# Pre-LN attention and gated feed-forward on one core: LN1 on ScalarE in three batches, exps of three and two banks, x of the tail loaded early

## The chip, the core and the metric

One core of a Trainium2 chip runs the kernel. Its engines work side by side, each through its own list of instructions in order: TensorE (PE) multiplies matrices out of the on-chip memory into eight accumulator banks, ScalarE (ACT) computes functions such as exp, VectorE (DVE) does elementwise work and reductions, GpSimd (POOL) general work, and SyncE (SP) issues DMA transfers. They wait for one another on semaphores. The metric is the device time of one execution in microseconds (us).

## The reference

x has 2,048 rows of 640 numbers in bf16. There are 32 heads of 20 numbers each; the feed-forward is 1,728 wide.

```python
h  = x + softmax_attention(layernorm(x) @ wqkv, heads=32, scale=20 ** -0.5) @ wo
n  = layernorm(h)
h2 = h + (gelu_tanh(n @ w_gate) * (n @ w_up)) @ w_down
layernorm(x) = (x - mean) / sqrt(var + 1e-5)
```

The softmax runs over all 2,048 keys. The output is h2.

## The kernel before

**The scheduler.** The kernel builds its whole program as a list of operations. Each has an engine, an assumed duration, a priority, its inputs and outputs and the accumulator banks that it takes and gives back (`op`, line 44). `schedule` (line 72) then plays the list through with the assumed durations: whenever an engine is free it takes the ready operation of the smallest priority number, and within one priority the one that was written first. What comes out is one fixed order per engine, and `emit` writes it down with the semaphore waits that it needs. On the chip each engine follows that order, whatever the true durations are. The priorities are `P_QK` 0 (scores, exps), `P_PV` 1 (products with the values), `P_EPI` 2 (epilogue) and `P_BG` 3 (everything in the background). Because all operations are recorded by one helper, most of them have line 257 in the profile.

**Head.** Sixteen tiles of 128 rows of x are loaded; `ln_stats` (line 400) takes mean and variance of each on DVE. After eight tiles `ln_rsqrt` (line 410) computes 1 / sqrt(var + eps) for them on DVE by a shift and two Newton steps. `ln_apply` (line 432) normalises a tile, five of each eight on POOL and three on DVE, into one of six slots. `transposes` (line 437) turns the tile on PE (five matmuls against the identity) and copies it out on ACT. POOL also spreads the weights of K and Q into padded arrays. `proj` (line 483) then makes K and Q of a group of four heads: five matmuls, a copy out of the bank, a square, a column sum on PE, for K a maximum, for Q a shift by half of K's maximum. `proj_v` makes the values. All of this has priority `P_BG`.

**Attention.** Queries come in five chunks: three of 512 (chunks 0 to 2) and two of 256 (chunks 3 and 4). Within a chunk the kernel goes over eight groups of four heads and over the keys. A tile is one bank of scores, 128 keys by 512 columns: one head and one key tile with 512 queries, or two key tiles with 256. `unit` (line 561) takes several tiles: the scores of all of them on PE, one exp over all their banks on ACT, and the products with the values on PE, which gather in bank 6. In chunk 0 a unit has two tiles, in banks 0, 1 or 2, 3 in turn; in all others three, in banks 0 to 2 or 3 to 5:

```python
units = [tiles[i:i + 2] for i in range(0, n2, 2)] + [tiles[i:i + 3] for i in range(n2, len(tiles), 3)]
```

In chunk 0 the projections of the other groups run in the background, in banks 7, 4 and 5. `epilogue` (line 614) takes a finished group out of bank 6, transposes it on PE in a background bank and divides by the sum of the exps.

**After a chunk.** `post` (line 637) takes the finished chunk: it loads x again (line 257, SP), transposes the attention output, multiplies by wo (line 478), adds x (line 655), normalises (LN2, again `ln_stats`, `ln_rsqrt`, `ln_apply`), and runs the feed-forward: gate and up matmuls (line 678), gelu from a tanh on ACT and several DVE steps, down matmuls (line 722), residual (line 726), store. It works in the background of the next chunk's units, at `P_BG` except for the first transposes, and in bank 7 alone. For the last chunk (`tail`) there is no next chunk: all eight banks are open and gelu is one ACT function (line 690).

Of the kernel before, what the change touches and what calls it, by code (L numbers as in the profile page):

```python
# [5 lines left out]
ACT = mybir.ActivationFunctionType  # L6
ALU = mybir.AluOpType
# [228 lines left out]
def bass_sequential_preLN__mha_block__glu_gated_geglu__prompt_kernel(  # L236
# [12 lines left out]
    with ExitStack() as es:  # L249
# [27 lines left out]
        rs = sb("rs", [128, NT], FP32)  # L277
        mu = sb("mu", [128, NT], FP32)
# [6 lines left out]
        qt_all = sb("qt_all", [128, NG, S])  # L285
# [10 lines left out]
        E_WORDS = 20820  # L296
# [26 lines left out]
        xn_p = carve(6 * D).rearrange("p (i d) -> p i d", i=6)  # L323
# [86 lines left out]
        def ln_rsqrt(t0, n, prio):  # L410
# [7 lines left out]
            d(I("tensor_scalar", sd16[:, 0:n], mv16[:, 0:n, 1], LN_EPS, None, ALU.add), ["mv16"], ["sd16"])  # L418
            d(I("tensor_copy", a, sd16[:, 0:n]), ["sd16"], ["nw0"])
            d(I("tensor_scalar", b.bitcast(I32), a.bitcast(I32), 1, None, ALU.logical_shift_right), ["nw0"], ["nw1"])  # L420
            d(I("tensor_copy", mu[:, t0:t0 + n], mv16[:, 0:n, 0]), ["mv16"], [("mu", t) for t in ts])
# [380 lines left out]
```

## Time and profile before

| | |
|---|---|
| runs, median (range) | 1109.22 us (1107.15 to 1115.55), three runs |
| the profiled execution | 1110.14 us, its span 1108.0 us |
| mean granted PE clock | 0.897 |
| ACT busy | 981.9 us, 89% |
| PE busy | 979.5 us, 88% |
| DVE busy | 438.2 us, 40% |
| POOL busy | 44.4 us, 4% |
| chain that ended last | ACT 55%, PE 37%, DVE 3%, POOL 3%, DMA 1% |

The span runs from the first to the last instruction of the profiled execution; the time of the execution lies a little above it. Busy is the time in which an engine works on at least one instruction. The chain that ended last is followed back from the last instruction, at each step to what released it. The granted clock is PE's, as a share of full speed.

### The profile page before, as it was taken

How to read it: one execution, taken by the hardware profiler on the slowest of the kernel's cores; microseconds unless marked ns; L12 is line 12 of the kernel's file. 1: busy time of each engine (PE TensorE's matmuls, PEld its weight loads, DVE VectorE, ACT ScalarE, POOL GpSimd, SP SyncE). 2: the span in 40 equal slices, each digit the busy share in tenths (PEclk: the TensorE clock that was granted, in tenths of full speed). 3: DMA queues.
4: the chain of work that ended last, by engine and by line, in shares of the span. 5: the costliest groups of instructions: out<-in, count | busy, mean ns of one | idle time of the engine just before them, and what ended most of it. 6: DMA issues, size and time to landing. Idle time of an engine off the chain costs nothing.

```text
span 1108.0 us, 16649 instructions
## 1 busy us (share of the span) xinstructions
PE 979.5 (88%) x7340; PEld 327.9 (30%) x7340; DVE 438.2 (40%) x917; ACT 981.9 (89%) x851; POOL 44.4 (4%) x47
## 2 busy tenths in 40 slices
PE   0599999999988998988899999988898989989768
PEld 0333332222222222331132222321132223333346
DVE  6344545555634555110035554110045554134532
ACT  0379999999889999999998999999999999999611
POOL 8700000000000000000000000000000000000000
PEclk9899999999978999995576999985589999998979
DMA  5000000000060000000000000000000000000000
GB/s 213 1 12 1 1 1 1 1 1 1 1 240 13 1 1 1 12 25 1 1 12 1 1 1 1 13 24 1 1 13 2 1 1 1 14 25 1 1 24 13
DMA packets 11832, 18.84 MB, mean 17 GB/s; under 512 B 688, under 2 KB 9840, under 8 KB 11760
## 3 DMA queue, kind: packets, MB, share of 16 engines
q1 hardware_dynamic: 11760, 17.78, 4.5%
q8 instruction: 57, 0.93, 0.4%
q14 instruction: 15, 0.12, 0.0%
HBM read 15.16 MB, written 2.62 MB: 16 GB/s over the span
## 4 chain that ended last, share of the span: by engine, by line
ACT 55%; PE 37%; DVE 3%; POOL 3%; DMA 1%; issue 0%; POOLq 0%; SPq 0%
ACT pts L257 53%; PE ps L257 17%; PE ps L478 10%; PE ps L678 4%; POOL rege L257 2%; ACT rege L257 2%; PE ps L513 2%; PE ps L722 2%; PE ps L624 1%; PE ps L441 1%; DMA rege<-in_A_wqkv_dram 1%; DVE rege L257 1%; POOL regw L257 1%; DVE rege L693 1%; DVE rege L709 0%
## 5 line engine op out<-in xcount | busy, mean ns | idle before, releaser
L257 ACT ACTIVATE pts<-ps 128x1536 bf16<-128x1536 f32 (+1 forms) x768 | 942.3, 1382 | 23.2 <-PE ps L257 19.9
L257 PE MATMUL ps<-qt_all,kt_all 32*128 32x512 bf16 (+1 forms) x2560 | 327.7, 374 | 55.7 <-ACT pts L257 53.2
L257 PE MATMUL ps<-pts,v_all 128*21 128x512 bf16 (+1 forms) x2560 | 286.5, 376 | 1.0 <-DVE osb L257 0.9
L678 PE MATMUL ps<-rege,regw 128*128 128x512 bf16 (+2 forms) x700 | 161.8, 350 | 18.8 <-DVE rege L693 6.5
L257 PEld LDWEIGHTS ps<-qt_all,kt_all 32*128 32x128 bf16 x2560 | 77.8, 93 | 309.7 <-ACT pts L257 237.2
L478 PE MATMUL ps<-regw 128*128 128x512 bf16 (+1 forms) x480 | 137.4, 368 | 0.0
L257 PEld LDWEIGHTS ps<-pts,v_all 128*21 128x21 bf16 x2560 | 65.8, 90 | 175.6 <-issue 164.6
L678 PEld LDWEIGHTS ps<-rege,regw 128*128 128x128 bf16 (+1 forms) x700 | 56.8, 101 | 86.8 <-issue 27.7
L722 PE MATMUL ps<-regw,rege 128*128 128x320 bf16 x448 | 80.6, 303 | 0.9 <-DVE rege L707 0.8
L257 DVE COPY osb<-ps 128x512 f32<-128x512 f32 (+1 forms) x40 | 23.3, 582 | 142.9 <-PE ps L257 142.9
L257 DVE SCALAR_TENSOR_TENSOR rege<-rege 128x512 bf16<-128x512 bf16 (+2 forms) x98 | 67.5, 689 | 20.9 <-ACT rege L257 19.3
L693 DVE CAST rege<-ps 128x512 bf16<-128x512 f32 (+1 forms) x49 | 33.8, 690 | 71.0 <-PE ps L678 70.8
L726 DVE TENSOR_TENSOR rege<-ps,rege 128x320 bf16<-128x320 f32 x32 | 15.7, 491 | 114.3 <-PE ps L722 114.2
L478 PEld LDWEIGHTS ps<-regw 128*128 128x128 bf16 x480 | 38.9, 101 | 57.1 <-issue 46.1
L709 DVE SCALAR_TENSOR_TENSOR rege<-rege,ps 128x512 bf16<-128x512 bf16 (+1 forms) x49 | 33.6, 686 | 46.5 <-PE ps L678 46.2
L722 PEld LDWEIGHTS ps<-regw,rege 128*128 128x128 bf16 x448 | 37.2, 98 | 37.3 <-issue 22.6
L447 ACT ACTIVATE regw<-ps 128x640 bf16<-128x640 bf16 x16 | 10.7, 703 | 39.8 <-PE ps L441 39.8
L441 PE MATMUL ps<-ident,rege 128*128 128x128 bf16 x80 | 10.8, 298 | 37.1 <-DVE mv L257 18.8
L257 ACT ACTIVATE rege<-rege 128x512 f32<-128x512 bf16 (+1 forms) x49 | 35.2, 719 | 8.7 <-DVE rege L257 8.5
L624 PE MATMUL ps<-identf,osb 128*128 128x128 f32 x128 | 33.5, 344 | 2.5 <-DVE osb L257 1.3
L524 DVE SCALAR_TENSOR_TENSOR qt_all<-ps,khalf,qt_all 128x512 bf16<-128x512 f32 x32 | 24.0, 750 | 21.1 <-PE ps L513 21.1
L540 DVE CAST v_all<-ps 128x320 bf16<-128x320 f32 x32 | 15.7, 492 | 42.0 <-PE ps L478 42.0
(62 smaller groups left out, 426.0 us busy)
## 6 DMA issues: line engine op xcount, KB each, us to landing
rege<-in_A_x_dram SPq DMA_DIRECT2D x4, 640.0 KB, 6.2
rege<-in_A_x_dram SPq DMA_DIRECT2D x16, 160.0 KB, 2.2
out_dram<-rege SPq DMA_DIRECT2D x16, 160.0 KB, 1.8
regw<-in_B_w_gate_dram SPq DMA_DIRECT2D x1, 2160.0 KB, 7.9
regw<-in_B_w_up_dram SPq DMA_DIRECT2D x1, 2160.0 KB, 12.8
regw<-in_B_w_down_dram SPq DMA_DIRECT2D x1, 2080.0 KB, 17.5
rege<-in_A_wqkv_dram SPq DMA_DIRECT2D x1, 1600.0 KB, 11.1
regw<-in_A_wqkv_dram SPq DMA_DIRECT2D x1, 800.0 KB, 12.5
```

What stands on the lines that cost most here:

```text
L257: return lambda eng: getattr(eng, method)(*args, **kwargs)
L441: op("pe", lambda eng, a=a: eng.transpose(bank16(bk, D)[:, 128 * a:128 * a + 128], src[:, a * 128:(a + 1) * 128], ident[:]), c_mm(128), pr ...
L478: yield op("pe", lambda eng, l=l, r=r, k=k: eng.matmul(bank(bk, n), l, r, start=(k == 0), stop=(k == len(steps) - 1)), c_mm(n), prio, read ...
L513: op("pe", lambda eng: eng.matmul(bank(b2), gm[:], sq[:, sqi, :], start=True, stop=True), c_mm(512), prio, reads=[("sq", sqi), "gq", "gqh" ...
L524: op("dve", lambda eng: eng.scalar_tensor_tensor(out=dst, in0=bank(b2), scalar=khalf[:, g:g + 1], in1=dst, op0=ALU.add, op1=ALU.add), c_dv ...
L540: op("dve", lambda eng: eng.tensor_copy(dst, src()), c_dve(320), prio, reads=[key], writes=[("v", kt, hf)], rel=[bk])
L624: op("pe", lambda eng, tt=tt: eng.transpose(bank(b2)[:, tt * 128:(tt + 1) * 128], osb[:, s, tt * 128:(tt + 1) * 128], identf[:]), c_mm(128 ...
L678: op("pe", lambda eng, a=a, f=f, fi=fi, mf=mf: eng.matmul(bank(bk)[0:mf, fi * nq:(fi + 1) * nq], w[:, a, f * 128:f * 128 + mf], hnT[:, a, ...
L693: op("dve", lambda eng, bg=bg, g16=g16, m=m: eng.tensor_copy(g16, bank(bg)[0:m, :]), c_dve(512), p, reads=[kg], writes=[("gb", i)], rel=[b ...
L709: fn = lambda eng, bu=bu, g16=g16, fv=fv, m=m: eng.scalar_tensor_tensor(out=fv, in0=g16, scalar=0.5, in1=bank(bu)[0:m, :], op0=ALU.mult, o ...
L722: op("pe", lambda eng, f=f, mf=mf, o=o, hf=hf, bk=bk: eng.matmul(bank(bk, 320), ha_f[0:mf, o:o + 128], wd[0:mf, f, hf * 320:(hf + 1) * 320 ...
L726: op("dve", lambda eng, bk=bk, tt=tt, hf=hf, i=i: eng.tensor_tensor(ob[:, i, hf * 320:(hf + 1) * 320], bank(bk, 320), h_sb[:, tt, hf * 320 ...
```

## The change

LN1 is done in three batches, of 4, 4 and 8 tiles. The square root of each batch is an ACT function, followed by a reciprocal on DVE and a product that gives minus mean over deviation. The first two batches are applied on ACT (one function with a scale and a bias per row), the third on DVE; POOL applies none. The slots for normalised tiles go from six to four. LN1, and K and Q of the first group of heads, have priority `P_EPI`.

Units of the last two chunks take three and two tiles in turn, in banks 0 to 2 and 3 to 4, and `post` and `epilogue` that run beside them have banks 7 and 5.

Q is stored by chunk, and the scratch of the gelu takes the place of chunk 0's Q; so `post` of chunk 0 also waits for that chunk's last scores. For the last chunk x is loaded once, into a buffer of its own, as soon as LN1 is done, and its part up to LN2 has priority `P_EPI`; LN2's Newton steps stay.

```diff
-        qt_all = sb("qt_all", [128, NG, S])
+        nm = sb("nm", [128, NT], FP32)
+        qt_all = sb("qt_all", [128, 4, NG, 512])
...
-        xn_p = carve(6 * D).rearrange("p (i d) -> p i d", i=6)
+        xn_p = carve(4 * D).rearrange("p (i d) -> p i d", i=4)
...
+        xr2 = carve(2 * D).rearrange("p (i s) -> p i s", i=2)
+        carve = carver(qt_all[:, 0, :, :].rearrange("p g s -> p (g s)"), NG * 512)
         th = carve(4 * 512).bitcast(FP32).rearrange("p (i s) -> p i s", i=2)
         zb = carve(2 * 512).rearrange("p (i s) -> p i s", i=2)
         gb = carve(2 * 512).rearrange("p (i s) -> p i s", i=2)
...
-        def ln_rsqrt(t0, n, prio):
+        def ln_rsqrt(t0, n, prio, need_nm=False):
...
+            if need_nm:
+                op("act", I("activation", sd16[:, 0:n], sd16[:, 0:n], ACT.Sqrt), 0.25, prio, reads=["sd16"], writes=["sd16"])
+                d(I("reciprocal", y, sd16[:, 0:n]), ["sd16"], rk)
+                d(I("scalar_tensor_tensor", out=nm[:, t0:t0 + n], in0=y, scalar=-1.0, in1=mu[:, t0:t0 + n],
+                    op0=ALU.mult, op1=ALU.mult), rk + [("mu", t) for t in ts], [("nm", t) for t in ts])
+                return
...
+            if eng == "act":
+                fn = I("activation", dst, src, ACT.Identity, bias=nm[:, t:t + 1], scale=rs[:, t:t + 1])
...
-        for i in range(2):
-            for t in range(8 * i, 8 * i + 8):
+        for t0, n, eng in ((0, 4, "act"), (4, 4, "act"), (8, 8, "dve")):
+            for t in range(t0, t0 + n):
                 ln_stats(x_sb[:, t, :], t, [f"x{t // 4}"], P_BG)
-            ln_rsqrt(8 * i, 8, P_BG)
-            for t in range(8 * i, 8 * i + 8):
-                eng = "pool" if t % 8 < 5 else "dve"
-                e_ops.append(ln_apply(eng, x_sb[:, t, :], xn_p[:, t % 6, :], ("xnp", t % 6), t, [f"x{t // 4}"], P_BG))
-                transposes(xn_p[:, t % 6, :], [("xnp", t % 6)], xnT[:, :, t * 128:(t + 1) * 128], ("xnT", t),
-                           ALLB, P_BG, "act")
+            ln_rsqrt(t0, n, P_EPI, True)
+            for t in range(t0, t0 + n):
+                e_ops.append(ln_apply(eng, x_sb[:, t, :], xn_p[:, t % 4, :], ("xnp", t % 4), t, [f"x{t // 4}"], P_EPI))
+                transposes(xn_p[:, t % 4, :], [("xnp", t % 4)], xnT[:, :, t * 128:(t + 1) * 128], ("xnT", t),
+                           ALLB, P_EPI, "act")
...
+        PAT = [((0, 1), (2, 3))] + [((0, 1, 2), (3, 4, 5))] * 2 + [((0, 1, 2), (3, 4))] * 2
...
+        while i < len(tiles):
+            pat = PAT[tiles[i][0]]
+            bs = pat[len(units) % 2]
+            units.append(tiles[i:i + len(bs)])
+            ubank.append(bs[0])
+            i += len(bs)
...
-            s0 = (2 if small else 3) * (u % 2)
+            s0 = ubank[u]
...
-            p = P_BG
+            p = P_EPI if tail else P_BG
...
-            first = tuple(e_ops) if c == 0 else ()
+            first = tuple(e_ops) + (last_qk0[0],) if c == 0 else ()
+            last = c == len(CHUNKS) - 1
...
-                op("sp", I("dma_start", xr[:, i, :], x_hbm[t * 128:(t + 1) * 128, :]), 0.08, p,
-                   writes=[("ob", i, 0), ("ob", i, 1)], sem=f"xr{i}", lat=2.5, after=first)
+                if not last:
+                    op("sp", I("dma_start", xr[:, i, :], x_hbm[t * 128:(t + 1) * 128, :]), 0.08, p,
+                       writes=[("ob", i, 0), ("ob", i, 1)], sem=f"xr{i}", lat=2.5, after=first)
+                elif tt == 0:
+                    op("sp", I("dma_start", xr2, x_hbm[q0:q0 + nq, :].rearrange("(i p) d -> p i d", p=128)), 0.08, p,
+                       writes=[("xr2", ii, jj) for ii in range(2) for jj in range(2)], sem="xr2", lat=2.5,
+                       after=tuple(e_ops))
...
+            p = P_BG
             hk = [("hnT", tt) for tt in range(nt)]
...
-        BG1 = (7,)
-        BG0 = (7, 4, 5)
+        BG = [tuple(b for b in (7, 5, 4) if b not in PAT[c][0] + PAT[c][1]) for c in range(len(CHUNKS))]
+        BG0 = BG[0]
...
-            proj("k", 0, c, PRO, P_BG, "act")
-        proj("q", 0, 0, PRO, P_BG, "act")
+            proj("k", 0, c, PRO, P_EPI, "act")
+        proj("q", 0, 0, PRO, P_EPI, "act")
...
-            post(c, ALLB if tail else BG1, tail)
+            post(c, ALLB if tail else BG[c + 1], tail)
```

## Rows read from the trace of the kernel before

**Rows 1.** Windows by stage: us, busy (instructions) by engine, granted PE clock, DMA

```profile
0.00:65.40 65.40, 27.98 (x155) 14.95 (x156) 31.22 (x104) 15.27 (x23) 44.44 (x47) 0.90 0.27 96
65.40:306.00 240.60, 238.99 (x1474) 71.48 (x1474) 128.47 (x231) 233.14 (x247) 0.00 (x0) 1.00 0.00 1
803.00:813.00 10.00, 10.00 (x96) 3.79 (x91) 2.46 (x6) 8.79 (x7) 0.00 (x0) 0.50 0.01 2
803.00:1042.90 239.90, 217.21 (x2530) 79.53 (x2525) 103.08 (x228) 236.51 (x189) 0.00 (x0) 0.96 0.02 7
1042.90:1108.00 65.10, 47.35 (x334) 32.36 (x332) 21.65 (x52) 9.13 (x14) 0.00 (x0) 0.87 0.05 16
```

**Rows 2.** Timeline of the head: start, us, engine, line, operation, count [idle before]

```profile
5.10 1.28 DVE L257 BATCH_NORM_STATS2 stats<-rege 128x6 f32<-128x320 bf16 x3 [1.36 <-DMA rege<-in_A_x_dram]
...
8.97 0.84 DVE L257 BATCH_NORM_STATS2 stats<-rege 128x6 f32<-128x320 bf16 x2
...
40.67 13.07 POOL L257 TENSOR_SCALAR rege<-rege,mu,rs 128x640 bf16<-128x640 bf16 x5 [4.90 <-DVE rs L257]
...
53.80 0.72 PE L441 MATMUL ps<-ident,rege 128*128 128x128 bf16 x5 [1.03 <-POOL rege L257]
...
54.55 1.90 ACT L447 ACTIVATE regw<-ps 128x640 bf16<-128x640 bf16 x3 [1.90 <-PE ps L441]
```

**Rows 3.** Timeline from the last normalised tile to the first exp

```profile
58.12 0.59 ACT L498 ACTIVATE qt_all<-ps 128x512 bf16<-128x512 f32 x1
...
60.40 0.69 ACT L495 ACTIVATE kt_all<-ps,e 128x512 bf16<-128x512 f32 x1 [1.68 <-PE ps L478]
...
61.12 0.42 DVE L257 TENSOR_TENSOR sq<-kt_all 128x512 bf16<-128x512 bf16 x1
...
62.03 0.69 DVE L516 TENSOR_REDUCE kmx<-ps 128x1 f32<-128x512 f32 x1
...
65.37 15.08 ACT L257 ACTIVATE pts<-ps 128x1024 bf16<-128x1024 f32 x16 [4.28 <-PE ps L257]
```

**Rows 4.** The chain that ended last, an undisturbed stretch: start, us, what

```profile
443.46 57.47 ACT pts L257 x43
```

**Rows 5.** Timeline of the tail

```profile
1045.18 0.32 DVE L632 TENSOR_TENSOR o_nat<-ps,rc 128x160 bf16<-128x160 f32 x1
...
1063.40 2.18 PE L722 MATMUL ps<-regw,rege 128*128 128x320 bf16 x14
...
1070.05 0.89 DVE L655 TENSOR_TENSOR rege<-ps,rege 128x320 bf16<-128x320 f32 x2 [2.38 <-DMA rege<-in_A_x_dram]
...
1072.14 0.17 DVE L257 CAST mv<-mv 128x4 bf16<-128x4 f32 x1
...
1074.73 0.80 DVE L257 TENSOR_SCALAR xn_t<-rege,mu,rs 128x640 bf16<-128x640 bf16 x2
...
1077.30 1.28 ACT L690 ACT_TABLE_LOAD   x1
...
1077.34 18.59 PE L678 MATMUL ps<-rege,regw 128*128 128x256 bf16 x140 [0.86 <-ACT rege L447]
```

**Rows 6.** Groups of the head: line, operation, count, busy, mean ns, idle before

```profile
L478 PE MATMUL ps<-regw 128*128 128x512 bf16 (+1 forms) x66 | 18.4, 420 | 0.0
```

**Rows 7.** The chain within the first chunk

```profile
106.56 0.65 PE ps L257 x6
107.21 0.32 PE ps L478
...
109.89 0.54 PE ps L478 x2
```

**Rows 8.** Groups of the tail

```profile
L678 PE MATMUL ps<-rege,regw 128*128 128x256 bf16 (+1 forms) x174 | 23.9, 300 | 4.9 <-ACT rege L257 2.6 <-ACT rege L447 0.9 <-DVE rege L709 0.8
...
L722 PE MATMUL ps<-regw,rege 128*128 128x320 bf16 x112 | 17.9, 308 | 0.8 <-DVE rege L707 0.8
```

**Rows 9.** Timeline where the first 256-query chunk begins

```profile
808.13 1.45 ACT L257 ACTIVATE pts<-ps 128x1536 bf16<-128x1536 f32 x1 [0.28 <-PE ps L257]
```

More of the change, by code (lines that the diff above doesn't have):

```diff
@@ L30 @@
     __slots__ = ("i", "eng", "fns", "dur", "lat", "prio", "deps", "succ", "nd", "ready",
-                 "acq", "rel", "sem", "start", "fin", "pos", "know")
+                 "acq", "rel", "sem", "tag", "start", "fin", "pos", "know")
 class Sched:
@@ L47, in op @@
         o.eng, o.dur, o.lat, o.sem = eng, dur, lat, sem
+        o.tag = writes[0] if writes else None
         o.fns = fns if isinstance(fns, list) else [fns]
@@ L418, in ln_rsqrt @@
             d(I("tensor_scalar", sd16[:, 0:n], mv16[:, 0:n, 1], LN_EPS, None, ALU.add), ["mv16"], ["sd16"])
+            d(I("tensor_copy", mu[:, t0:t0 + n], mv16[:, 0:n, 0]), ["mv16"], [("mu", t) for t in ts])
+            if need_nm:
[4 more added lines that the diff above has]
+                return
             d(I("tensor_copy", a, sd16[:, 0:n]), ["sd16"], ["nw0"])
             d(I("tensor_scalar", b.bitcast(I32), a.bitcast(I32), 1, None, ALU.logical_shift_right), ["nw0"], ["nw1"])
-            d(I("tensor_copy", mu[:, t0:t0 + n], mv16[:, 0:n, 0]), ["mv16"], [("mu", t) for t in ts])
             d(I("tensor_scalar", y.bitcast(I32), b.bitcast(I32), -1.0, RSQRT_MAGIC, ALU.mult, ALU.add), ["nw1"], rk)
@@ L483, in proj @@
         def proj(which, g, c, banks, prio, evac="dve"):
-            wp, all_, nm = (wk_pad, kt_all, "k") if which == "k" else (wq_pad, qt_all, "q")
+            wp, nm = (wk_pad, "k") if which == "k" else (wq_pad, "q")
             wkey = ("wkp" if which == "k" else "wqp") + ("0" if g == 0 else "")
-            dst = all_[:, g, c * 512:(c + 1) * 512]
+            dst = kt_all[:, g, c * 512:(c + 1) * 512] if which == "k" else qt_all[:, c, g, :]
             bk = Bank(*banks)
@@ L548, in bass_sequential_preLN__mha_block__glu_gated_geglu__prompt_kernel @@
             tiles += [(c, g, kb, j) for g in range(NG) for kb in range(NT // nk) for j in range(4)]
+        PAT = [((0, 1), (2, 3))] + [((0, 1, 2), (3, 4, 5))] * 2 + [((0, 1, 2), (3, 4))] * 2
         n2 = 64 * NG
-        units = [tiles[i:i + 2] for i in range(0, n2, 2)] + [tiles[i:i + 3] for i in range(n2, len(tiles), 3)]
+        units, ubank = [], []
+        i = 0
+        while i < len(tiles):
[4 more added lines that the diff above has]
+            i += len(bs)
         ends = []
@@ L559, in bass_sequential_preLN__mha_block__glu_gated_geglu__prompt_kernel @@
         pv_wait = []
+        last_qk0 = [None]
         def unit(u):
@@ L620, in epilogue @@
                reads=[("O", c, g)], writes=[("osb", s)], rel=[bk])
-            b2 = Bank(*(BG0 if c == 0 else BG1))
+            b2 = Bank(*BG[c])
             key = ("bk", sc_id())
@@ L637, in post @@
         def post(c, banks, tail):
-            p = P_BG
+            p = P_EPI if tail else P_BG
             q0, nq = CHUNKS[c]
             nt = nq // 128
-            first = tuple(e_ops) if c == 0 else ()
+            first = tuple(e_ops) + (last_qk0[0],) if c == 0 else ()
+            last = c == len(CHUNKS) - 1
+            xrb, xk = (xr2, "xr2") if last else (xr, "ob")
             ev = "act" if tail else "dve"
@@ L655, in post @@
                     op("dve", lambda eng, bk=bk, tt=tt, hf=hf, i=i: eng.tensor_tensor(
-                        h_sb[:, tt, hf * 320:(hf + 1) * 320], bank(bk, 320), xr[:, i, hf * 320:(hf + 1) * 320], ALU.add),
-                       c_dve(320), p, reads=[key, ("ob", i, hf)], writes=[("h", tt, hf)], rel=[bk], after=first)
+                        h_sb[:, tt, hf * 320:(hf + 1) * 320], bank(bk, 320), xrb[:, i, hf * 320:(hf + 1) * 320], ALU.add),
+                       c_dve(320), p, reads=[key, (xk, i, hf)], writes=[("h", tt, hf)], rel=[bk], after=first)
                 ln_stats(h_sb[:, tt, :], t, [("h", tt, 0), ("h", tt, 1)], p)
```

19 lines of the change are left out of this document (11 added, 8 removed).

## The prediction

> **What bounds the kernel now.** The page's totals have ScalarE (ACT) and TensorE (PE) each busy for nearly nine tenths of the span, and an average over unlike stages cannot say which limits, so I read the table by stage first [rows 1]. Until 65.4 us ACT is busy 15.3 us: no exp has started. From 65.4 to 306 (queries 0 to 511, exps of two banks) ACT works 233.1 of 240.6 us and PE 239.0. From 803 to 1042.9 (the two 256-query chunks) ACT works 236.5 of 239.9 us, PE 217.2. After the last exp 65.1 us remain, with ACT at 9.1 and PE at 47.4. So there are a head that waits, a stretch in which PE and ACT are level, one in which ACT leads and PE has 22.7 us idle, and a tail that waits.
>
> Next the order of time in the head: the chain runs through GpSimd (POOL). Five LN1 applies there take 13.07 us, in two such groups, and the last three transposed tiles are evacuated only at 54.55 + 1.90 = 56.45 [rows 2]. From there to the first exp at 65.37 it is a chain of small steps [rows 3]. In the middle the chain of waits is ACT's own: 43 exps of three banks in 57.47 us, 1.3365 each [rows 4]. In the tail PE first does the feed-forward left over from the chunk before, DVE waits for x, a chain of 14 short DVE operations follows, and the last feed-forward starts at 1077.34 [rows 5].
>
> **The change, part by part.** The sum is made against the profiled execution: span 1108.0, time 1110.14; the median of the three runs is 0.9 lower.
>
> *LN1 (removes ten POOL applies and the Newton steps).* When is the last tile normalised? DVE's statistics start at 5.1 us, when x lands, and nine halves (4.5 tiles) on it is 8.97: 0.86 us a tile [rows 2], so 13.8 for sixteen. Three square-root groups of five short DVE operations at 0.19, the pitch in the tail ((1074.73 - 1072.14) / 14 [rows 5]), add 2.8. Two squares and maxima of K (0.42 + 0.69 each [rows 3]), which now go ahead of statistics, add 2.2. The last group is ready at 5.1 + 13.8 + 2.8 + 2.2 = 23.9; a hop to ACT for the square root and back, 0.7, makes 24.6. Eight tiles follow at the pace of their slowest step, five transposes in about 0.7 (0.72 for five; evacuations three in 1.90 [rows 2]); the first also needs its apply, 0.5, and the last its evacuation, 0.7. So 24.6 + 0.5 + 8 x 0.7 + 0.7 = 31.4, instead of 56.45.
>
> An apply of 640 elements on ACT, with a scale and a bias read from memory, is not in the trace. Low end: an evacuation of 640 elements without them, 0.6 back to back. High end 0.8: K's evacuation with one such operand takes 0.69, Q's without one 0.59 [rows 3], so 0.1 an operand. I take 0.8, the nearer row. Eight are 6.4 us, 16 evacuations 9.6, K's and Q's 3: 19 us between about 10 and 34, which fits with little room. The ends move the head by 0 to 2 us.
>
> From the last tile on: five matmuls of Q's and K's width at 0.22 and hops are 1.3 us; from the last K evacuation at 60.40 to the first exp at 65.37 the trace has 4.97 [rows 3]. The 4 us between 56.45 and 60.40 were mostly other matmuls, which now stand behind. So the first exp comes at 31.4 + 1.3 + 5.0 = 37.7, say 38, instead of 65.4: **minus 27.4**. Ends: 33 and 46.
>
> Square root and exp bring a second function table. The one load that the trace shows amid the work takes 1.28 us and starts as ACT's earlier work ends, beside the first matmuls of the group whose results ACT waits for [rows 5]. One more, between Q's evacuation and the first exp, falls into a wait of 3 us or more: 0, at most 1.28. The Trainium skill (ScalarE: Activation LUTs, What ACT_TABLE_LOAD costs) has about 2.66 us for a switch with its drain against the row's 1.28; by its figure the uncovered end would be 1.4 us higher.
>
> *What PE did meanwhile.* By 65.4 it had done 66 projection matmuls [rows 6]; K and Q of the first group are 25 of them, so 41 others, mostly V, stood beside the POOL wait. At 0.155 us (14 of V's width in 2.18 [rows 5]) they are 6.4 us. In the shorter head about half may find room; the rest goes into the stretch after, where PE is level with ACT: **plus 3.5** (0 to 7).
>
> *Exps of 3 and 2 banks in turn.* 2,048 tiles make 768 exps now and 802 after, 34 more, all in the last two chunks. On ACT five tiles cost 1.3365 x 5/3 = 2.2275 now and 1.3365 + p after; the pace p of a two-bank exp lies between 0.89 (two thirds of 1.3365: no fixed part) and 0.94 (240.6 / 256, with PE in the way). I take the middle, 0.917: 102 pairs make 2.6 us (0 to 5). On PE a unit pays 0.65 for scores and products; a background burst takes 0.32 for one matmul and 0.54 for two, so 0.10 for the interruption [rows 7]. 34 units add 34 x 0.75 = 25.5 us against PE's idle of 22.7. ACT then wants 236.5 + 2.6 = 239.1, PE 217.2 + 25.5 = 242.7, just the longer: 242.7 for 239.9, **plus 3** (0 to 12).
>
> *Second bank for the background.* Now bank 7 alone serves the feed-forward and the epilogue's transposes, and a group waits for DVE to evacuate the one before. With bank 5 the next can start. But by the last paragraph PE has no idle left, so I count no faster background: 0, and about the same leftover at the last exp.
>
> *Tail.* Normalisation and output projection of the last chunk go ahead of the leftover. The chunk's own chain from the last exp at 1042.9: epilogue to 1045.5, 2.6; ten transposes 1.4, evacuations 1.3; ten projection matmuls 1.5; residual, statistics and square root 4.7 (1070.05 to 1074.73); applies 0.8, transposes 0.7, evacuation 0.7, hops 0.6: 14.3, against 1077.34 - 1042.9 = 34.4. Beyond that group's 140 matmuls and the last 56, PE still does 34 and 56 after the last exp [rows 8]: at 18.59 / 140 and 2.18 / 14 [rows 5] 4.5 + 8.7 = 13.2 us. With 4.4 of the chain's own PE work that overfills 14.3 by 3. So **minus 17** (0 if the leftover still goes first; 22 if it is gone and the group's slow first matmuls are too).
>
> *The x load* leaves SP's queue in the tail and is issued once, behind LN1; behind it stand only chunk 0's x and the weights, both wanted near 300 us. The DVE wait that it removes, 2.38 us [rows 5], is inside the 17. *Costed at nothing:* scratch moved into chunk 0's queries (its first user waits for that chunk's products anyway, which come after its scores); four slots instead of six for normalised tiles (a slot comes free with its transposes; without that cover the tile pitch grows by an apply, 8 x 0.5 = 4 us); Q's new order.
>
> Sum: -27.4 + 3.5 + 3 - 17 = -37.9. **1110.1 - 37.9 = 1072.2**; from the median 1071.3. I say 1072.
>
> **The rivals.**
> 1. *PE sets the pace of the last two chunks and the background falls behind.* For it: 25.5 us of new PE work against 22.7 of room. If 10 us are lost there and the tail stays: 1110 - 27.4 + 3.5 + 10 = 1096; with half the tail's gain 1088. Against it: two banks make fewer waits. The Trainium skill (TensorEngine Tiling (Array Packing), Key Properties) says that a change of tiling mode drains the engine, so that more, smaller units are more drains; by that rule this rival, and the bursts' fixed 0.10 agrees. Chance 0.20, at 1083 to 1097.
> 2. *Slower: PE's clock.* From 803 to 813, right after a stretch without background, the granted clock was 0.50, 1.2 GHz [rows 1], and a unit with a burst took 1.45 + 0.28 = 1.73 us, ACT waiting [rows 9]. If the last two chunks stay at that level, 204 units are 353 us instead of 240: 1110 + 113 - 41 = 1182. It decides from a mean of (240 + 41 + 11) / 204 = 1.43 us a unit, most of them at half clock. Against it: 0.96 over both chunks, and PE gets more to do, not less. Chance 0.04.
> 3. *The head stays.* A static order that puts a statistics step or an evacuation behind a wait of another engine could keep the first exp at 55; with rival 1's losses: 1110 - 10 + 5 - 5 = 1100. For it: sixteen tiles' work of ACT and DVE in order fills both. Against it: with POOL gone no single step is over 1 us. Chance 0.07.
> 4. *Better throughout:* first exp at 33, little lost in the middle, tail minus 22: 1110 - 32 + 3 - 22 = 1059 or less. Chance 0.09.
>
> **How the numbers follow.** The forecast (1060 to 1083) has 0.60. The range 1058 to 1092 takes it in, with over half of rival 1 and half of rival 4: some 0.78. Under 1% (11 us) a change can hardly be told from none: faster by more 0.90 (forecast, rivals 1 and 4, a little of 3), within it 0.05, slower 0.05.
>
> **What would show it.** POOL done near 23 us; the last normalised tile evacuated near 31, the first exp near 38; three table loads, the second before the first exp. Chunk 0's exps over 240 to 248 us. The last two chunks over 240 to 246 us, PE hardly idle. From the last exp to the end 48 us, the long feed-forward group starting 14 to 18 us in. Wrong would be a first exp after 46, last chunks over 250, a tail over 58.

## The result and the profile after

| | before | after |
|---|---|---|
| runs, median (range) | 1110.41 us (1107.15 to 1115.55), four runs | 1079.20 us (1077.46 to 1084.56), four runs |
| the profiled execution | 1110.14 us, span 1108.0 | 1080.92 us, span 1079.1 |
| mean granted PE clock | 0.897 | 0.899 |
| PE busy, ACT busy | 979.5, 981.9 us | 994.7, 995.2 us |

The ratio is 0.9723, with an interval from 0.9669 to 0.9777. The time lies within the range of 1058 to 1092 and 7 us above the 1072 forecast. The sum behind it is another matter: several of its terms were wrong, in both directions. The two profiled spans, cut at the first exp, at the end of each chunk's exps and at the last exp, give the terms one by one:

| stage | before | after | measured | forecast |
|---|---|---|---|---|
| head, to the first exp | 65.4 | 42.4 | -23.0 | -27.4 |
| chunk 0 | 249.4 | 244.2 | -5.2 | +3.5 |
| chunk 1 | 243.5 | 248.6 | +5.1 | 0 |
| chunk 2 | 242.3 | 243.5 | +1.2 | 0 |
| chunks 3 and 4 | 242.4 | 253.9 | +11.5 | +3 |
| tail, from the last exp | 65.1 | 46.6 | -18.5 | -17 |
| sum | 1108.0 | 1079.1 | -28.9 | -37.9 |

The windows of the kernel after, by those stages, answer to [rows 1]; the columns are the same (from, to, length; busy time and instructions of PE, PEld, DVE, ACT, POOL; granted clock; DMA share; GB/s):

```profile
0.00:42.40 42.40, 25.75 (x177) 14.50 (x178) 30.02 (x97) 22.81 (x35) 19.16 (x37) 1.00 0.44 147
42.40:286.60 244.20, 242.58 (x1496) 71.80 (x1494) 131.71 (x233) 242.08 (x256) 0.00 (x0) 1.00 0.01 3
286.60:535.20 248.60, 219.94 (x1394) 63.48 (x1394) 74.73 (x148) 238.52 (x186) 0.00 (x0) 0.82 0.09 32
778.70:911.70 133.00, 130.73 (x1266) 43.61 (x1266) 65.98 (x140) 124.91 (x117) 0.00 (x0) 0.89 0.01 4
911.70:1032.60 120.90, 117.62 (x1346) 47.80 (x1342) 42.10 (x98) 120.24 (x110) 0.00 (x0) 1.00 0.03 10
1032.60:1079.10 46.50, 36.77 (x273) 25.79 (x271) 16.26 (x43) 8.06 (x12) 0.00 (x0) 0.93 0.04 15
```

In chunk 3 PE is busy 130.73 of 133.0 us and ACT misses 8.1; in chunk 1 ACT misses 10.1 although PE is idle for 28.7, so there a wait of another kind sits. The head's timeline, which answers to [rows 2, 3], shows POOL gone from the chain and where the head lost the 4.4 us that the forecast had promised:

```profile
11.57 1.73 ACT L258 ACTIVATE rege<-rege,nm,rs 128x640 bf16<-128x640 bf16 x2 [0.72 <-DVE nm L258]
...
15.05 8.28 POOL L258 COPY regw<-rege 128x400 bf16<-128x400 bf16 x12 [1.55 <-DMA rege<-in_A_wqkv_dram]
...
17.32 2.56 PE L493 MATMUL ps<-regw 128*128 128x320 bf16 x9 [3.25 <-DMA regw<-in_A_wqkv_dram]
...
20.44 0.70 ACT L463 ACTIVATE regw<-ps 128x640 bf16<-128x640 bf16 x1 [4.01 <-PE ps L457]
21.04 0.20 ACT L258 ACTIVATE sd<-sd 128x4 bf16<-128x4 bf16 x1
21.27 0.18 DVE L258 RECIPROCAL rs<-sd 128x4 f32<-128x4 bf16 x1 [4.70 <-ACT sd L258]
...
29.78 2.94 DVE L258 TENSOR_SCALAR rege<-rege,mu,rs 128x640 bf16<-128x640 bf16 x8
30.76 4.88 ACT L463 ACTIVATE regw<-ps 128x640 bf16<-128x640 bf16 x8 [0.39 <-PE ps L457]
...
37.40 0.69 ACT L510 ACTIVATE kt_all<-ps,e 128x512 bf16<-128x512 f32 x1 [1.19 <-PE ps L493]
38.10 1.28 ACT L258 ACT_TABLE_LOAD   x1
42.37 1.02 ACT L258 ACTIVATE pts<-ps 128x1024 bf16<-128x1024 f32 x1 [2.98 <-PE ps L258]
```

Three engines stand for one transfer here. PE stands for 3.25 us, until 17.32, at a matmul of V (320 columns) whose weights have not landed, and the transposes that could run are behind it in PE's order. ACT waits 4.01 us for one of them, the second square root sits behind that evacuation on ACT, and DVE waits 4.70 us for the square root. From the last evacuation of K at 37.40 to the first exp at 42.37 it is 4.97 us, to the hundredth what [rows 3] had.

In the tail, the timeline that answers to [rows 5] has no wait for x, and the long feed-forward group starts 16.5 us after the last exp:

```profile
1034.73 0.32 DVE L658 TENSOR_TENSOR o_nat<-ps,rc 128x160 bf16<-128x160 f32 x1
...
1035.11 0.73 PE L457 MATMUL ps<-ident,o_nat 128*128 128x128 bf16 x10
...
1036.36 2.97 PE L493 MATMUL ps<-wo,rege 128*128 128x320 bf16 x20
...
1039.26 2.42 PE L756 MATMUL ps<-regw,rege 64*128 64x320 bf16 x15
...
1042.24 0.49 DVE L688 TENSOR_TENSOR rege<-ps,rege 128x320 bf16<-128x320 f32 x1
...
1046.53 0.80 DVE L258 TENSOR_SCALAR xn_t<-rege,mu,rs 128x640 bf16<-128x640 bf16 x2
...
1049.10 1.28 ACT L724 ACT_TABLE_LOAD   x1
1049.13 17.93 PE L712 MATMUL ps<-rege,regw 128*128 128x256 bf16 x140 [0.86 <-ACT rege L463]
...
1067.85 8.51 PE L756 MATMUL ps<-regw,rege 128*128 128x320 bf16 x56 [0.78 <-DVE rege L741]
```

After the last exp PE does 140 gate and up matmuls, all of them the last chunk's own, and 87 down matmuls, of which 31 are the chunk's before. In [rows 8] it was 34 and 56 left over. What removed that leftover is the question that the experiments answer.

### The profile page after: what moved, and what is told of

The parts are those of the page before. It is cut to its first block, busy times and chain, and to the rows that moved or that the text cites. A ratio compares the mean times of both kernels' runs of the same rounds, so it can differ in the third digit from the quotient of the medians.

```text
span 1079.1 us, 16678 instructions
## 1 busy us (share of the span) xinstructions
PE 994.7 (92%) x7340; PEld 330.8 (31%) x7340; DVE 435.1 (40%) x906; ACT 995.2 (92%) x897; POOL 19.2 (2%) x37
## 4 chain that ended last, share of the span: by engine, by line
PE 48%; ACT 46%; DMA 3%; DVE 3%; issue 0%; SPq 0%; DVEq 0%
ACT pts L258 44%; PE ps L258 23%; PE ps L493 11%; PE ps L712 6%; PE ps L756 3%; PE ps L457 2%; DMA rege<-in_A_x_dram 2%; ACT qt_all L258 2%; PE ps L528 2%; PE ps L650 2%; DMA regw<-in_A_wqkv_dram 1%; DVE qt_all L258 1%; DVE qt_all L727 1%; DVE rege L743 0%; SPq L258 0%
## 5 line engine op out<-in xcount | busy, mean ns | idle before, releaser
L258 PE MATMUL ps<-qt_all,kt_all 32*128 32x512 bf16 (+1 forms) x2560 | 342.6, 375 | 42.1 <-ACT pts L258 40.2
L258 PE MATMUL ps<-pts,v_all 128*21 128x512 bf16 (+1 forms) x2560 | 298.3, 377 | 0.5 <-DVE osb L258 0.4
L258 PEld LDWEIGHTS ps<-qt_all,kt_all 32*128 32x128 bf16 x2560 | 81.6, 93 | 302.1 <-ACT pts L258 212.4
L258 DVE COPY osb<-ps 128x512 f32<-128x512 f32 (+1 forms) x40 | 23.3, 582 | 141.2 <-PE ps L258 140.9
L258 DVE SCALAR_TENSOR_TENSOR qt_all<-qt_all 128x512 bf16<-128x512 bf16 (+2 forms) x98 | 67.2, 688 | 12.2 <-ACT qt_all L258 10.6
L727 DVE CAST qt_all<-ps 128x512 bf16<-128x512 f32 (+1 forms) x49 | 33.9, 691 | 69.0 <-PE ps L712 68.8
L760 DVE TENSOR_TENSOR rege<-ps,rege 128x320 bf16<-128x320 f32 x32 | 15.7, 492 | 111.3 <-PE ps L756 111.2
L743 DVE SCALAR_TENSOR_TENSOR rege<-qt_all,ps 128x512 bf16<-128x512 bf16 (+1 forms) x49 | 33.6, 687 | 44.3 <-PE ps L712 44.2
L493 PE MATMUL ps<-wo,rege 128*128 128x320 bf16 x160 | 32.2, 321 | 5.2 <-DVE rege L688 5.2
L258 ACT ACTIVATE qt_all<-qt_all 128x512 f32<-128x512 bf16 (+1 forms) x49 | 33.0, 674 | 1.0 <-DVE qt_all L258 0.8
L656 DVE RECIPROCAL rc<-ps 128x16 f32<-128x16 f32 (+1 forms) x40 | 9.5, 236 | 59.5 <-PE ps L650 59.5
L688 DVE TENSOR_TENSOR rege<-ps,rege 128x320 bf16<-128x320 f32 x32 | 15.7, 492 | 39.4 <-PE ps L493 32.2
```

What stands on the lines that cost most here:

```text
L258: return lambda eng: getattr(eng, method)(*args, **kwargs)
L493: yield op("pe", lambda eng, l=l, r=r, k=k: eng.matmul(bank(bk, n), l, r, start=(k == 0), stop=(k == len(steps) - 1)), c_mm(n), prio, read ...
L688: op("dve", lambda eng, bk=bk, tt=tt, hf=hf, i=i: eng.tensor_tensor(h_sb[:, tt, hf * 320:(hf + 1) * 320], bank(bk, 320), xrb[:, i, hf * 32 ...
L727: op("dve", lambda eng, bg=bg, g16=g16, m=m: eng.tensor_copy(g16, bank(bg)[0:m, :]), c_dve(512), p, reads=[kg], writes=[("gb", i)], rel=[b ...
L743: fn = lambda eng, bu=bu, g16=g16, fv=fv, m=m: eng.scalar_tensor_tensor(out=fv, in0=g16, scalar=0.5, in1=bank(bu)[0:m, :], op0=ALU.mult, o ...
L760: op("dve", lambda eng, bk=bk, tt=tt, hf=hf, i=i: eng.tensor_tensor(ob[:, i, hf * 320:(hf + 1) * 320], bank(bk, 320), h_sb[:, tt, hf * 320 ...
```

## Experiments

Each was timed against the kernel before on the same chip, and each has a profile. Stage lengths are those of one profiled execution, and they differ somewhat where nothing was changed: in the kernels below that leave the changed head alone it takes 41.6 to 42.4 us, and chunk 2 takes 238.2 to 244.9 in the kernels without the filler of experiment 5. The single repairs of experiments 3 to 5 gain 3 to 5 us on the kernel after, with intervals that overlap its own (0.9669 to 0.9777). So they are judged by the wait that each removes from the trace, and not by the total alone.

**1. One part at a time.** Three kernels start from the kernel before and take one part of the change each.

LN1 alone:

```diff
-            for t in range(8 * i, 8 * i + 8):
-                eng = "pool" if t % 8 < 5 else "dve"
+        for t0, n, eng in ((0, 4, "act"), (4, 4, "act"), (8, 8, "dve")):
+            ln_rsqrt(t0, n, P_EPI, True)
```

> The kernel before with the LN1 part alone (batches of 4, 4 and 8, square roots and two batches on ACT, priority for LN1 and the first K and Q). Theory A, the stages add up: first exp at 42 us, chunk 0 about 244 us long, the last two chunks 242 and the tail 65 as before; in all 28 us less, 1082. Rival B, the head's gain is given back in chunk 0 by projections that were not done early: first exp at 42, chunk 0 longer than 249, 1090 or more.

Measured: 1084.2 us, ratio 0.9748 (0.9693 to 0.9804). Stages: head 42.0, chunk 0 244.2, chunk 1 244.0, chunks 3 and 4 242.1, tail 67.1. Theory A holds: the head and the shorter chunk 0 are the LN1 part's; chunk 1 is not lengthened by it. The tail, whose code is the same as before, takes 67.1 instead of 65.1, so a difference of 2 us there says little by itself.

The tail part alone (priority of the last `post`, x loaded early into its own buffer):

```diff
-            p = P_BG
+            p = P_EPI if tail else P_BG
...
+                    op("sp", I("dma_start", xr2, x_hbm[q0:q0 + nq, :].rearrange("(i p) d -> p i d", p=128)), 0.08, p,
```

> The kernel before with the tail's part alone (priority of the last chunk's normalisation and output projection, its x loaded early). Theory A: the tail goes from 65 to about 47 us without the second background bank, everything else as before, 1092. Rival C, the tail is short only because two banks leave less over: it stays above 58 us, 1103 or more.

Measured: 1107.72 us, ratio 0.9977 (0.9950 to 1.0005); tail 62.6 instead of 65.1: no clear gain in all, and rival C holds (above 58 us, 1103 or more). The wait for x of 2.38 us is gone from the trace and little else. The tail's timeline says why the priority did nothing:

```profile
1044.10 0.32 DVE L633 TENSOR_TENSOR o_nat<-ps,rc 128x160 bf16<-128x160 f32 x1
...
1050.54 1.92 PE L687 MATMUL ps<-rege,regw 128*128 128x256 bf16 x10 [2.63 <-ACT rege L257]
1052.40 1.25 PE L442 MATMUL ps<-ident,o_nat 128*128 128x128 bf16 x10
...
1061.70 0.49 DVE L735 TENSOR_TENSOR rege<-ps,rege 128x320 bf16<-128x320 f32 x1 [1.75 <-PE ps L731]
1062.22 0.49 DVE L663 TENSOR_TENSOR rege<-ps,rege 128x320 bf16<-128x320 f32 x1
...
1067.23 0.49 DVE L735 TENSOR_TENSOR rege<-ps,rege 128x320 bf16<-128x320 f32 x1 [1.75 <-PE ps L731]
1067.75 0.49 DVE L663 TENSOR_TENSOR rege<-ps,rege 128x320 bf16<-128x320 f32 x1
```

The attention output is normalised at 1044.4, and its transposes (L442) come at 1052.40, right behind the leftover's last gate and up matmuls (L687). The residual sums (L663) stand one for one behind those of the leftover (L735). The reason is in the code: the transposed attention output is written where the chunk before keeps its normalised rows, which those matmuls still read, and the residual sum goes into the rows of `h_sb` that the leftover's L735 still reads. A priority cannot move work ahead of the readers of the place that it writes.

The units alone (three and two tiles, banks 7 and 5 for the background):

```diff
+        PAT = [((0, 1), (2, 3))] + [((0, 1, 2), (3, 4, 5))] * 2 + [((0, 1, 2), (3, 4))] * 2
...
-        BG1 = (7,)
-        BG0 = (7, 4, 5)
+        BG = [tuple(b for b in (7, 5, 4) if b not in PAT[c][0] + PAT[c][1]) for c in range(len(CHUNKS))]
```

> The kernel before with exps of three and two banks in turn in the two 256-query chunks and the second background bank there, alone. Theory A: the last two chunks take 252 to 254 instead of 242 us, and the second bank pulls some of the leftover out of the tail (65 to about 60): 1110 plus 5 to 10. Rival D, more units cost PE nothing that matters and the long chunk 3 of the changed kernel has another cause: 242 to 245 us for the two chunks, a shorter tail, 1103.

Measured: 1107.72 us, ratio 0.9972 (0.9941 to 1.0003). Chunks 3 and 4 take 255.0 us, 12.6 more, and the tail takes 49.0, 16.1 less; its leftover is 0 and 31, as after the whole change. Theory A had the chunks right, but the tail is shorter than its 60 us and the total not 5 to 10 us longer. So the units and the second bank shorten the tail, by clearing the leftover before the last exp, and pay for nearly all of it in the chunks.

**2. The second bank taken back.** The whole change, units of three and two, but bank 5 not given to the background:

```diff
-        BG = [tuple(b for b in (7, 5, 4) if b not in PAT[c][0] + PAT[c][1]) for c in range(len(CHUNKS))]
+        BG = [tuple(b for b in ((7, 5, 4) if c == 0 else (7,)) if b not in PAT[c][0] + PAT[c][1]) for c in range(len(CHUNKS))]
```

> The changed kernel with its exps of three and two banks, but bank 5 not given to the background. Theory A, the units cost PE and the bank only moves work: the last two chunks shorter than with the bank (246 to 250), a longer tail by 3 to 6, within 4 us of the changed kernel in all. Rival G, the second bank is what makes PE late: last two chunks back at 245 and the whole 5 us faster or more.

Measured: 1126.62 us, ratio 1.0138 (1.0085 to 1.0191), slower than before. The windows of its chunk 3, chunk 4 and tail, and the groups of the tail:

```profile
774.50:910.60 136.10, 126.49 (x1199) 38.83 (x1209) 51.04 (x114) 123.58 (x112) 0.00 (x0) 0.81 0.01 4
910.60:1032.90 122.30, 116.57 (x1252) 41.16 (x1257) 39.67 (x95) 119.42 (x108) 0.00 (x0) 0.96 0.03 10
1032.90:1121.60 88.70, 67.22 (x416) 44.03 (x413) 34.73 (x73) 11.87 (x19) 0.00 (x0) 0.77 0.02 8
```

```profile
L712 PE MATMUL ps<-rege,regw 128*128 128x256 bf16 x238 | 40.0, 340 | 9.4 <-DVE qt_all L727 3.9 <-DVE rege L743 3.9 <-ACT rege L463 0.9
...
L712 PE MATMUL ps<-rege,regw 128*64 128x256 bf16 x20 | 4.0, 348 | 0.0
```

The leftover is 258 - 140 = 118 gate and up matmuls and 56 down matmuls. It runs after the last exp with one bank, and PE waits for DVE between its groups. Chunks 3, 4 and tail together take 347.1 us against 300.4 after: the bank that I had counted at nothing is worth 47 us to a kernel with these units. Neither expectation came near. The leftover is made by the plan and not on the chip: each engine's order is fixed before the run, and in chunks 3 and 4 of this kernel PE waits for DVE only 2.4 us in all. `schedule` passes over a group while its only bank is taken and goes on with units. That this is what piles up the leftover is read from the code; no run times it by itself.

The other way round, three tiles in every unit of the last two chunks, so that the background has bank 7 alone as before:

```diff
-  [((0, 1, 2), (3, 4))] * 2
+  [((0, 1, 2), (3, 4, 5))] * 2
```

> The changed kernel with exps of three banks in the last two chunks as before, so bank 7 alone for the background; head, tail and x as changed. Theory A: the last two chunks take 242 instead of 254 us and the tail grows by the leftover, 47 to 50 or 52: 6 to 9 us faster than the changed kernel, 1071 to 1073. Rival D: no faster, since the second bank pays for itself.

Measured: 1082.22 us, ratio 0.9743 (0.9700 to 0.9786). Chunks 3 and 4 take 244.2, the tail 62.6, leftover 34 and 56 as before. Theory A had the chunks right and the tail wrong (47 to 52 expected); rival D holds. Against the whole change's 1079.20 the pair of units and bank is worth some 3 us net, with intervals that overlap.

**3. The place that is written twice.** If the reuse of places holds the tail back, giving the last chunk rows of its own should free it. Its rows and columns are moved by two tiles, into places that chunk 3 does not use:

```diff
+            ro = 2 if last else 0
-  oT[:, a, tt * 128:(tt + 1) * 128]
+  oT[:, a, (tt + ro) * 128:(tt + ro + 1) * 128]
-  h_sb[:, tt, ...]
+  h_sb[:, tt + ro, ...]
```

On the whole change:

> The changed kernel, but the last chunk keeps its residual rows in tiles 2 and 3 of h and its transposed outputs in columns 256 to 511, which the chunk before (256 queries) doesn't use. Theory J, the last chunk's path waits for the leftover not for want of priority but because both write the same places: its transposes wait for the leftover's gate and up matmuls, its residual for the leftover's stores. After the last exp 31 down matmuls are left, about 5 us; so the tail goes from 46.6 to 43 to 45 us, 2 to 3 us less in all, 1076 to 1077. Rival K, priority decides: tail within 1 us of 46.6.

Measured: 1076.26 us, ratio 0.9678 (0.9633 to 0.9723); tail 43.6 instead of 46.6, within the 43 to 45 expected.

On the kernel of three-tile units:

> The changed kernel with exps of three banks in the last two chunks (bank 7 alone for the background, leftover of 34 feed-forward and 56 down matmuls) and the last chunk's rows and columns apart. Theory J: without the shared places the priority works; the tail goes from 62.6 (three-bank exps, shared places) to 50 to 54 us, with the second bank not needed for it, and the whole to 1070 to 1074. Rival K: tail still above 60.

Measured: 1075.64 us, ratio 0.9674 (0.9626 to 0.9723); tail 54.8 instead of 62.6, with the same leftover of 34 and 56 matmuls; expected were 50 to 54, and 1070 to 1074 in all. So where a leftover exists, 7.8 us of the tail were the wait for its places. The distance to 43.6 is 11.2 us; the 34 gate and up and 25 down matmuls more make some 8.4 of it, an estimate from [rows 5] (18.59 / 140 and 2.18 / 14 each), and the rest was not traced. With the places apart the two kinds of unit cost about the same: chunks 3, 4 and tail are 298.5 us with three and two, 295.7 with three.

**4. Where chunk 1 and the head lose.** After's chain of waits at the start of chunk 1, and its timeline there:

```profile
285.29 19.02 DMA rege<-in_A_x_dram
...
304.41 0.50 DVE rege L688
```

```profile
304.41 0.49 DVE L688 TENSOR_TENSOR rege<-ps,rege 128x320 bf16<-128x320 f32 x1 [6.98 <-DMA rege<-in_A_x_dram]
...
304.95 1.52 PE L493 MATMUL ps<-wo,rege 128*128 128x320 bf16 x5 [5.17 <-DVE rege L688]
...
307.06 1.45 ACT L258 ACTIVATE pts<-ps 128x1536 bf16<-128x1536 f32 x1 [5.35 <-PE ps L258]
```

A load of 160 KB takes 19.02 us from its issue. It waits for chunk 0's last scores now; by then the 6.4 MB of feed-forward weights have been issued, and it stands behind them in the queue. DVE waits for it, PE waits for DVE to free a bank, and ACT waits 5.35 us for scores that are behind PE's matmul. Loading x right after LN1 again, without the wait for the scores (it does not touch the scratch):

```diff
-                       ... sem=f"xr{i}", lat=2.5, after=first)
+                       ... sem=f"xr{i}", lat=2.5, after=tuple(e_ops) if c == 0 else ())
```

> The changed kernel, but the x loads of chunk 0's second part wait for LN1 alone and no longer for chunk 0's last scores. Theory A: the loads are then ahead of the weights in the queues; the wait of 19 us for x behind the weights goes, with 5.3 us of ACT waiting in it; chunk 1 from 248.6 to 243.5, 5 us less in all, 1074. Rival E, the transposes and the clock at chunk 1's start cost this time whatever x does: within 2 us of the changed kernel.

Measured: 1073.89 us, ratio 0.9666 (0.9605 to 0.9728); chunk 1 takes 243.7 instead of 248.6. The wait for scores at 307 is gone, while the other kernels whose load is as late have it too (4.3 to 5.8 us at the same place in experiments 2, second kernel, and 3). So the 5 us are that load's.

The Trainium skill (DMA: Bandwidth & Descriptors, Queues, rings and completion order) states that each DMA engine takes a queue's descriptors in ring order. This trace agrees: x was issued last, at 285.29, and landed at 304.31, as the weights ended.

For the head, the scheduler was told that V's weights land late, so that it plans transposes ahead of V's matmuls:

```diff
-load(wv, ..., "wv", 0.8)
+load(wv, ..., "wv", 3.5)
```

> The changed kernel, with the planner told that the V weights land about 11 us later than it assumes (near 17 us, where the trace has them), so that no V matmul stands ahead of the transposes of the first tiles. Theory A: PE no longer stands 3.3 us waiting for the V weights with transposes, evacuations and the second square root behind it; the first exp comes 3 to 5 us earlier, at 37.5 to 39.5, 1075 to 1077. Rival F, DVE's statistics set the head anyway: first exp within 1 us of 42.4.

Measured: 1074.50 us, ratio 0.9675 (0.9638 to 0.9713); head 39.6 instead of 42.4, just outside the 37.5 to 39.5 expected. The third square root comes at 25.16 instead of 28.81. The two kernels of experiment 6, with the same plan for V, have 39.0 and 39.6. So 2 to 3 of the 4.4 us that the head fell short were that wait.

**5. The clock at the start of a chunk.** Towards the end of chunks 1 and 2 the background has run out. In the kernel after, the granted clock is 0.50 (1.2 GHz) there, with PE busy 4.2 to 4.9 of each 5 us and ACT hardly losing anything, and it is still there when the next chunk's background starts. Eighty-four matmuls of 512 columns into bank 7, whose results nothing reads, were put into the ends of chunks 1 and 2:

```diff
+            if c in (0, 1):
+                for _ in range(84):
+                    op("pe", lambda eng, bk=bk: eng.matmul(bank(bk), ident[:], wo[:, 0, 0:512], start=True, stop=True), ...
```

> The changed kernel with 84 extra matmuls of 512 columns into bank 7, read by nobody, in the stretch without background work at the end of chunk 1 and again of chunk 2 (work added, none removed). Theory H, the slow start of chunk 3 is PE at half clock, which it has when the background work comes back: the granted clock stays at 1.0 over the start of chunks 2 and 3, both start without ACT waiting, chunk 3 takes 125 to 128 us instead of 133, and the whole is 6 to 10 us faster. Rival I, chunk 3 is long because its units ask too much of PE at any clock: chunk 3 within 2 us of 133.

Measured: 1075.67 us, ratio 0.9701 (0.9650 to 0.9752), mean granted clock 0.965; chunk 2 239.1 instead of 243.5, chunk 3 128.3 instead of 133.0. By the length of chunk 3 that is near theory H, though the whole is 3.5 us faster and not 6 to 10. The windows show what the clock did. Stretches of 5 us around the start of chunk 3, first of after (with one of its second fall), then of this kernel:

```profile
778.70:783.70 5.00, 4.77 (x38) 1.64 (x38) 0.69 (x1) 4.59 (x4) 0.00 (x0) 0.50 0.00 0
783.70:788.70 5.00, 5.00 (x45) 1.62 (x39) 1.24 (x3) 3.91 (x3) 0.00 (x0) 0.50 0.00 0
788.70:793.70 5.00, 5.00 (x41) 2.16 (x40) 1.48 (x3) 3.51 (x4) 0.00 (x0) 0.50 0.02 3
...
823.70:828.70 5.00, 5.00 (x38) 1.11 (x36) 0.76 (x2) 2.58 (x4) 0.00 (x0) 0.54 0.00 0
```

```profile
770.00:775.00 5.00, 3.56 (x32) 0.92 (x31) 0.00 (x0) 5.00 (x5) 0.00 (x0) 1.00 0.00 0
775.00:780.00 5.00, 4.36 (x44) 1.54 (x44) 0.69 (x1) 4.64 (x5) 0.00 (x0) 0.71 0.00 0
780.00:785.00 5.00, 5.00 (x45) 1.73 (x40) 1.24 (x3) 4.22 (x4) 0.00 (x0) 0.50 0.01 3
785.00:790.00 5.00, 5.00 (x54) 2.18 (x53) 1.69 (x4) 3.75 (x4) 0.00 (x0) 0.77 0.00 0
```

The filler holds the clock at 1.00 to the end of chunk 2, and when chunk 3's background starts it falls to 0.50 all the same. But the filler itself had run out: the last of it in the trace starts at 771.77, 3 us before chunk 3, and PE is busy 3.56 of 5 us from 770 to 775, where under the filler it was 4.3 to 4.6. So theory H had the clock right at chunk 2 and wrong at chunk 3, and whether the thin stretch or the denser work behind it brings the clock down is open. In the first kernel of experiment 6, with the same filler, the clock is at 0.50 for 15 us and chunk 3 takes 132.4. Units of three and two gave a chunk 3 of 129.0 to 133.1 us without the filler and of 128.3 and 132.4 with it, so its length shows no gain. At the start of chunk 2, where the filler lasts to 0.4 us before the chunk, the clock is 1.00 throughout; the kernel after has 0.50 for some 15 us, and its ACT loses 2.2 us in the first 20. A gain from that is not shown either: the kernel with x early has no filler, starts chunk 2 at 0.50 and 0.61, and takes 238.2 us for it. The interval overlaps that of after.

**6. The repairs together.** x early, V's weights planned late, the filler and rows apart, with units of three and two:

> The changed kernel with four repairs together: x of chunk 0 ahead of the weights, V weights planned late, filler matmuls before chunks 2 and 3, the last chunk's rows and columns apart. If they add up: head 39.6, chunk 1 244, chunk 2 239, chunk 3 128, chunk 4 122, tail 44, chunk 0 245: 1062 to 1066.

Measured: 1069.18 us (1056.76 to 1071.55, six runs), ratio 0.9585 (0.9534 to 0.9637), above the 1062 to 1066 expected; chunk 3 took 132.4 where 128 was counted on. With units of three tiles throughout and bank 7 alone:

> The same four repairs, and exps of three banks throughout, so without the second background bank. Theory J with theory A: the last two chunks 242 to 244 instead of 250 us, the tail 50 to 54 instead of 44: within 4 us of the kernel with exps of three and two banks. Rival G, the second bank is needed: 8 us slower than it or more.

Measured: 1064.94 us (1060.57 to 1069.96, six runs), ratio 0.9577 (0.9538 to 0.9617). Its windows of chunk 3, chunk 4 and tail:

```profile
764.00:885.70 121.70, 107.38 (x1233) 36.69 (x1247) 62.70 (x134) 121.03 (x99) 0.00 (x0) 0.97 0.02 4
885.70:1005.30 119.60, 107.50 (x1301) 43.29 (x1300) 41.20 (x95) 117.55 (x93) 0.00 (x0) 0.96 0.03 10
1005.30:1058.80 53.50, 44.07 (x334) 30.05 (x332) 20.96 (x52) 9.18 (x14) 0.00 (x0) 0.97 0.04 13
```

The stages came about as expected (241.3 and 53.5 against 242 to 244 and 50 to 54), and rival G is out. Both kernels beat the kernel after, with intervals that do not meet its own; they cannot be told from each other. The three-tile kernel gives the tail 53.5 us and takes 241.3 for the two chunks, where the other takes 255.4 and 44.9.

## Why the prediction was right, and where its steps failed

**Head, forecast -27.4, measured -23.0: right mechanism, short by 4.4.** POOL ended at 23.3 (near 23 forecast), the eight last tiles took 0.61 us each (0.7 taken), and the step from K's evacuation to the first exp was 4.97 as taken. What failed is the time of the last group: the third square root came at 28.81 where the sum had about 24, and the last tile was out at 35.64 instead of 31.4. I had added up DVE's work and never asked what PE's order puts ahead of the transposes. A load's wait there costs everything behind it; 2 to 3 us of it were taken back by planning V later, the rest was not traced. The applies on ACT were 0.91 each and 0.82 apart (1.73 for two), a little above the 0.8 that I took: 7.0 us for the eight instead of 6.4. The table load before the first exp cost nothing, as costed: it ran at 38.10 for 1.28 us, beside a wait of 2.98.

**Chunk 0, forecast +3.5, measured -5.2: wrong sign.** I had argued that projections pushed out of the shorter head would be paid for here. They were not pushed out: PE did 88 projection matmuls before the first exp against the 66 of [rows 6], in 23 us less, because the head's work had been waiting. And ACT lost less: in this stretch of the kernel before it is busy 241.8 of 249.4 us, 7.6 short, after 242.1 of 244.2, 2.1 short. The cause was there to be read in ACT's timeline in chunk 0 of the kernel before:

```profile
284.40 6.52 ACT L257 ACTIVATE pts<-ps 128x1024 bf16<-128x1024 f32 x7 [4.26 <-PE ps L257]
```

With another of 0.87 us at 96.81 that makes 5.1 us in which the exps waited for PE; the kernel after has no such wait in chunk 0. A stretch that looks level by its busy shares held two stalls of order, and the new plan does not have them.

**Chunk 1, forecast 0, measured +5.1: an edit costed at nothing.** I wrote that moving the scratch into chunk 0's queries was free, since its first user waits for the chunk's products anyway. I followed the scratch and not the other thing that waits with it: `first` also holds back the two loads of x, and they land behind 6.4 MB of weights. For the tail's x load I named what stands behind it in the queue; for chunk 0's loads I did not ask what stands ahead. Experiment 4 shows the term whole.

**Units of three and two, forecast +3, measured +11.5, inside its range of 0 to 12.** By the prediction's own sign ("last chunks over 250") this step was wrong: they took 253.9. The pace on ACT was right. The chain of after late in chunk 3 has four pairs:

```profile
893.96 9.02 ACT pts L258 x8
```

That is 2.255 us a pair, against 1.3365 + 0.917 = 2.2535 taken. (The upper bound of 0.94 for that pace was misread: the 240.6 us of [rows 1] hold 247 exps and not 256, which makes 0.974; the value taken does not hang on it.) PE's busy time over the two chunks grew by 28.9 us, from 219.5 to 248.4, near the 25.5 of the sum; but part of that is leftover work that moved out of the tail, where PE is busy 10.6 us less, and part is the clock. What was too small is what PE's part costs, in chunk 3 above all: PE has no idle left there, so the two stretches at half clock are paid in full. ACT waits for PE 7.8 us in this chunk of after, nearly all of it in these stretches, where the kernel before had slack and lost 1.4. With the clock at 1.00 (chunk 4) the units cost 120.9 for 119.4. So about half of this term goes with rival 2's mechanism and not with the price of a unit; no run separates the two.

**Second bank, forecast 0, and tail, forecast -17: both wrong, in opposite directions.** The step that failed is the one that gave the tail's gain to priority and the early load. By experiment 1 these two give 2.5 us of tail and the units with their bank 16.1. By experiment 2 the bank carries it: with the same units and without it 118 and 56 matmuls are left over, with it 0 and 31. My argument that "PE has no idle left" treated PE's time as the only limit of the background; in the plan a group also has to wait until its bank has been emptied, and the second bank gives the next group a place. The priority could not do what the sum had it do, since the last chunk's path writes places that the leftover still reads (experiment 3). The tail came out near the forecast (46.6 against 48) by another route, and that is luck.

**Rivals.** Rival 1, PE setting the pace of the last chunks, is what chunk 3 shows (133.0 us for 123.0), yet its second half, a leftover that stays, did not come. Rival 2's mechanism is real, at 0.50 for the first 15 us of chunk 3 and again near 820, and far from deciding. Rival 3's kind of wait held the head by 4 us, not by that rival's 17. The forecast was right in size by luck: the errors, +4.4 for the head, -8.7 for chunk 0, +6.3 for chunks 1 and 2, +8.5 for the last two and -1.5 for the tail, cancel to 9.

## What to carry to other kernels

Before giving a step priority, look for who still reads the place that it writes: a reused buffer orders two pieces of work more firmly than any priority, and giving it another place is the cheaper edit. When an edit adds a wait to a list of conditions, follow everything that shares the list, and ask of each transfer what is ahead of it in its queue at the new time. And accumulator banks are a resource of their own beside an engine's busy time: with the same units, one bank more or less decided whether 31 or 174 matmuls were left over for the tail.

## What the runs showed of the hardware

- An ACT apply of 128x640 with scale and bias read from memory took 0.91 us alone and 0.82 back to back. The Trainium skill (ScalarE: Activation LUTs, What ACT_TABLE_LOAD costs) gives about 186 ns plus 0.833 ns a column, 93 ns for each operand read from memory, and an overlap of 93 ns between neighbours: an estimate by that page of 905 and 812 ns, and the trace agrees.
- Time and mean granted clock go together in the six runs of experiment 6's first kernel, from 1056.76 us at 0.981 to 1071.55 us at 0.959. It is not so in every kernel: the one with three tiles in every unit (experiment 2) took 1078.76 us at 0.907 and 1083.12 us at 0.908.
- The clock can be low while PE has much to do: in the kernel after it was 0.50 from 480 to 535 us with PE busy 4.2 to 4.9 of each 5 us. And it can fall as PE gets more to do: in the filler kernel PE was busy 3.56 of 5 us at 1.00, as the filler had run out, then 4.36 and 5.00 in the two stretches in which the granted clock went to 0.71 and 0.50. At the start of chunk 2 of the same kernel it was busy 3.75 of 5 us from 535 to 540, and the clock stayed at 1.00. What sets the fall off is not settled by these runs.
